# Another order for the opening of a spectral and gated-ReLU kernel

## The chip, the cores and the metric

The kernel runs on one core of one Trainium2 chip. The metric is the device time of one execution in microseconds (us), the median of several runs. A profiled execution gives a trace of every instruction on the five engines: TensorE (PE, with its weight loads as PEld), VectorE (DVE), ScalarE (ACT), GpSimd (POOL) and SyncE (SP), which here issues nearly all transfers. An engine works its instructions in the order in which the program has them, and each may wait on semaphores for others.

## The reference

For one sequence of 2048 rows of 448 numbers, the result is the input plus two branches, both on the layer-normalized rows:

```python
def _A_ref(x, w_r, w_i):
    X = jnp.fft.rfft2(x, axes=(-2, -1))
    X = X * (w_r + 1j * w_i)
    return jnp.fft.irfft2(X, s=(S, D), axes=(-2, -1))

def _B_ref(x, W_gate, W_up, W_down):          # W_gate, W_up: 448 x 1792, W_down: 1792 x 448
    gate = jnp.einsum("bsd,df->bsf", x, W_gate)
    up = jnp.einsum("bsd,df->bsf", x, W_up)
    gate = gate * (gate > 0)
    return jnp.einsum("bsf,fd->bsd", gate * up, W_down)

xn = _layernorm(x, axis=-1)
return x + _A_ref(xn, A_w_r, A_w_i) + _B_ref(xn, B_W_gate, B_W_up, B_W_down)
```

Everything is float32. The kernel keeps that precision with float16 matmuls: each operand is split into a high half (the value rounded to float16) and a low half (the rest), and a product is the sum of high x high, high x low and low x high.

## The kernel before

**Rows.** A tile is 128 rows, number `n2` of 16 (row 16 p + n2 on partition p). A chunk is four of them, `q`, `q + 4`, `q + 8`, `q + 12`; the chunks are taken in the order 0, 2, 1, 3. Each row tile is loaded (`load_xr`, "lx"), its mean and variance are taken on VectorE (`ln_stats`, "st": BN_STATS and BN_AGGR), the root on ACT (`ln_sd`, "sq"), and the reciprocal of the root with one refining step as four or five tiny operations on VectorE (`ln_rstd`, "rs"). In the two first chunks VectorE writes the normalized row in float32 (`ln_xn`, "xn", line 290) and also its low half (`ln_lo`, "lo", lines 324 and 325). The high half (`ln_hi`, "hi") is made by ACT; in chunk 0 straight from the raw row (line 297), in chunk 2 from the normalized one (line 299). GpSimd copies a few columns into place (`ln_copy`, "cp", and the last line of `ln_lo`, line 326). Chunk 0 is then transposed by TensorE against an identity (`ln_tp`, "tpA" and "tpB", line 344) and emptied into the tile T by VectorE (line 352, "vev") or ACT (line 350, "aev"). The other chunks are transposed by transfers (`ln_dma`, "dm", line 334), a transfer for each row tile; these go through SP's queue.

**Weights.** Gate and up weights come in 14 pairs `f`; each pair has two slabs, `g` = 0 (gate) and 1 (up), of 128 columns. A slab is loaded ("lw"), squared and summed by ACT (`w_sq`, "wsq", line 186), summed over the partitions by GpSimd (`w_sum`, "par", line 189), scaled by a power of two worked out by two tiny VectorE operations (`w_scale`, "wsc", lines 192 and 196), rounded to its high half by ACT (`w_hi`, "whi", line 690) and given its low half by VectorE (`w_lo`, "wlo", line 694). The down weights go the same way ("lwd", "wdq", "wdp", "wdsc", "wdh", "wdl").

**Units.** A unit is one `f` for one chunk: 20 full matmuls of 128x512 (line 740), ten to a slab, and two half passes (line 747). Two units in turn share their half passes: `gu_halves` ("hp") ends unit `f` and opens its mate, the next unit. Then come the relu on ACT ("re", line 777), the product on VectorE ("tm", line 781), and the high and low half of h ("gh", line 785, and "gl", line 789). A unit needs its PSUM tile, one of two, to be emptied by "tm" of the unit two before. When the five units of a group are done for a chunk, the matmuls with the down weights follow (line 808). The spectral branch (lines 368, 398, 639, 658 and VectorE's butterflies) is laid among the units by a planner with a list of costs.

**What sets the order.** The opening, all work up to the first chunk's five units, is written by hand: the string `OPENING` names some 280 pieces, and `manual_schedule` holds every engine to the order in which they are named. Unit 0 runs there in slabs of half a chunk (256 columns: "hh", "hl", "lh" with the slab and the half), as rows come in. `keep_warm` runs matmuls on a tile of zeros at the start and between early pieces ("warm", "kw1", "kw3", "kw6"). From there on a planner and the scheduler set the order.

Of the kernel before, what the change touches and what calls it, by code (L numbers as in the profile page):

```python
# [25 lines left out]
NWARM = 19  # L26
# [4 lines left out]
lx0 lx4 lw lid lw lx8 lx12 lw lw lw lw lx2 lx10 lx6 lx14 lwd0 lwd1 lwd2 lwd3 lwd4 warm st0 st4 sqA rsA hi4  # L31
xn4 xn0 wsqW0g0 cp4 st8 hi0 parW0g0 st12 wsqW0g1 cp0 tpA0 lo0 tpA4 kw1 wscW0g0 sqB tpB0 kw6 parW0g1 wsqW1g0
rsB whiW0g0 vevB0 lo4 wsqW1g1 xn12 tpB4 kw3 hi8 parW1 wscW0g1 xn8 whiW0g1 cp8 vevA0 vevA4 hi12 tpA8 vevB4
hh10 hh00 lo8 wsqW2g1 cp12 tpA12 hl00 lo12 aevA12 tpB8 aevA8 hl10 wloW0g0 lw aevB8 tpB12 wscW1 lh00 aevB12
wloW0g1 lw lfd hh01 hh11 whiW1g0 st2 lh01 lh10 whiW1g1 hl01 wloW1g0 lw hl11 wsqW2g0 wloW1g1 lw ly0 ly4 ly8
ly12 d90 d94 d98 d912 lh11 wsqW3g0 st10 parW2 hp0 st14 wsqW3g1 gu1g0 st6 wdq0 parW3 wscW2 sqC wscW3 whiW2g0 rsC gu1g1 re0
wloW2g0 whiW3g1 tm0 whiW2g1 xn6 wsqW4g0 xn2 gu2g0 wloW2g1 hi2 re1 xn10 gh0 wloW3g1 whiW3g0 tm1 gu2g1 wdq1
wloW3g0 hi10 xn14 lo2 hi14 hi6 cp14 hp2 wsqW4g1 cp2 lo6 gu3g0 cp10 dm2 lo14 re2 parW4 wdq2 cp6 wscW4 tm2
whiW4g0 dm14 lo10 wdq4 gu3g1 wloW4g0 gh1 dm10 gl0 whiW4g1 gl1 dm6 gu4g0 re3 wloW4g1 wdq3 tm3 wdp gh3
wdsc gh2 gu4g1 gl2 wdh1 wdh2 wdl1 wdh0 wdl2 hp4 gl3 re4 wdh3 tm4 wdl0 gh4 wdh4 gl4 wdl3 wdl4  # L40
# [105 lines left out]
def tile_gfnet_reglu(ctx: ExitStack, tc: tile.TileContext, x, xr, wgu, wd, wf, ident, c_fd, c_fm, c_im, c_row, c_id,  # L146
# [100 lines left out]
    def ln_stats(q, j):  # L247
        n2 = q + 4 * j
        st = ft([128, 6], F32, "bst", 2)
        V.bn_stats(st, xr_t[n2])  # L250
        if j == 0:
            mv[q] = ft([128, 4, 2], F32, "mv", 2)
        V.bn_aggr(mv[q][:, j, :], st)

    rst = {}

    def ln_sd(q, js=(0, 1, 2, 3)):
        w = ft([128, 5, 4], F32, "rs", 3)
        n = len(js)
        rst[q, js[0]] = w[:, :, 0:n], mv[q][:, js[0]:js[-1] + 1, :]  # L260
        A.activation(w[:, 0, 0:n], rst[q, js[0]][1][:, :, 1], AF.Sqrt, bias=eps)

    def ln_rstd(q, js=(0, 1, 2, 3), bias=False):
        w, m = rst[q, js[0]]
        sd, r0, t, r, nm = (w[:, i] for i in range(5))
        V.reciprocal(r0, sd)
        V.scalar_tensor_tensor(t, m[:, :, 1], 1e-5, r0, op0=OP.add, op1=OP.mult)
        V.scalar_tensor_tensor(t, t, -0.5 * 2048, r0, op0=OP.mult, op1=OP.mult)
        V.scalar_tensor_tensor(r, t, 1.5 * 2048, r0, op0=OP.add, op1=OP.mult)
        if bias:  # L270
            V.scalar_tensor_tensor(nm, m[:, :, 0], -1.0, r, op0=OP.mult, op1=OP.mult)
        elif q in CHUNKS[2:]:
            V.tensor_scalar(nm, m[:, :, 0], -1.0, None, op0=OP.mult)
        for i, j in enumerate(js):
            rst[q, j] = r[:, i:i + 1], nm[:, i:i + 1], m[:, i, 0:1]
# [9 lines left out]

    def ln_xn(n2):
        xn_b[n2] = free.pop(0)
        xn[n2] = xn_b[n2].rearrange("p g c k -> p (g c k)")[:, 0:D]
        r, _, mean = rst[n2 % 4, n2 // 4]
        V.tensor_scalar(xn[n2], xr_t[n2], mean, r, op0=OP.subtract, op1=OP.mult)  # L290

    def ln_hi(n2, fused=False):
        new_tt(n2)
        o = tt[n2].rearrange("p a b -> p (a b)")[:, 0:D]
        r, nm, _ = rst[n2 % 4, n2 // 4]
        if fused:
            A.activation(o, xr_t[n2], AF.Identity, scale=r, bias=nm)
        else:
            A.activation(o, xn[n2], AF.Copy)
# [6 lines left out]
    def ln_norm(n2):  # L306
        xn_b[n2] = free.pop(0)
        xn[n2] = xn_b[n2].rearrange("p g c k -> p (g c k)")[:, 0:D]
        r, nm, _ = rst[n2 % 4, n2 // 4]
        A.activation(xn[n2], xr_t[n2], AF.Identity, bias=nm)  # L310
        new_tt(n2)
        A.activation(tt[n2].rearrange("p a b -> p (a b)")[:, 0:D], xn[n2], AF.Copy, scale=r)
        ln_copy(n2)
        free.append(xr_b.pop(n2))

    def ln_lo(n2):
        x, t = xn[n2], tt[n2].rearrange("p a b -> p (a b)")
        x2, t2 = [v[:, None, :].to_broadcast([128, 2, 64]) for v in (x[:, 384:448], t[:, 384:448])]
        if n2 % 4 in CHUNKS[2:]:
            r = rst[n2 % 4, n2 // 4][0]  # L320
            V.scalar_tensor_tensor(t[:, 512:896], x[:, 0:384], r, t[:, 0:384], op0=OP.mult, op1=OP.subtract)
            V.scalar_tensor_tensor(tt[n2][:, 3:9:5, 64:128], x2, r, t2, op0=OP.mult, op1=OP.subtract)
        else:
            V.tensor_tensor(t[:, 512:896], x[:, 0:384], t[:, 0:384], op=OP.subtract)
            V.tensor_tensor(tt[n2][:, 3:9:5, 64:128], x2, t2, op=OP.subtract)
# [370 lines left out]
    def wd_sq(i, f):  # L696
        if i == 0:
# [45 lines left out]
    def gu_half(f, q, g, start, prev):  # L743
# [479 lines left out]
```

## Time and profile before

| | us |
|---|---|
| median of 3 runs | 447.49 (447.28 to 447.83) |
| the profiled execution: its own time | 448.09 |
| the profiled execution: span of its instructions | 446.3 |
| TensorE busy | 437.7 (98% of the span) |
| VectorE busy | 381.9 (86%) |
| ACT busy | 188.2 (42%) |
| granted TensorE clock, mean | 0.999 of full speed |

A row of the order of time reads: start, duration, engine, line and operation, tile written <- tiles read, shapes, how many in a row, and in brackets the idle time of the engine before it with what ended it. A row of a group reads: line, engine, operation, tiles, shapes, count, then busy time in all and the mean of one in ns, then idle time before. A row of windows gives each engine's busy time in a stretch with its count of instructions, the granted clock, the share of the transfer engines and GB/s. Instructions on one engine overlap a little at their ends, so a step from one to the next is some 0.05 to 0.1 us shorter than a duration.

### The profile page before, as it was taken

Reading aid. Unit: us, or ns where it says so; the run is one execution under the profiler, and the core shown is the slowest. Engines: PE = TensorE matmul, PEld = TensorE weight load, DVE = VectorE, ACT = ScalarE, POOL = GpSimd, SP = SyncE. Lnnn points to the kernel's source line nnn. Section 1 sums busy time; section 2 is a strip of 40 time slices with the busy share of each in tenths; the row PEclk is TensorE's granted clock in tenths of the full one; section 3 lists DMA queues with packets and bytes.
Section 4 is the critical chain, followed back from the end, with each engine's and each line's share of the span. In section 5 each row is a group of like instructions: output and inputs, shape, how many; then the busy total and the mean of one; then the engine's idle time right before and its main releaser. Section 6 shows DMA issues by size and latency. Waiting matters only on the chain.

```text
span 446.3 us, 7350 instructions
## 1 busy us (share of the span) xinstructions
PE 437.7 (98%) x2625; PEld 219.1 (49%) x2625; DVE 381.9 (86%) x958; ACT 188.2 (42%) x398; POOL 34.3 (8%) x89
## 2 busy tenths in 40 slices
PE   6999999999999999999999999999999999999996
PEld 2544555545455444444444444444445555555654
DVE  5989698999858899999999999987998799875443
ACT  5887263732643774323132255263334133244130
POOL 2320030210000310000000310100000000000000
PEclk9999999999999999999999999999999999999999
DMA  7939985040001462431302100011121121101212
GB/s 248 312 88 269 368 266 116 16 92 2 1 2 48 140 198 81 133 117 45 98 29 85 41 0 2 0 43 63 41 71 35 58 79 35 53 13 50 82 47 82
DMA packets 39228, 39.61 MB, mean 89 GB/s; under 512 B 18470, under 2 KB 35096, under 8 KB 39192
## 3 DMA queue, kind: packets, MB, share of 16 engines
q1 hardware_dynamic: 39192, 39.15, 28.6%
q8 instruction: 20, 0.33, 0.3%
q14 instruction: 16, 0.13, 0.1%
HBM read 24.38 MB, written 3.67 MB: 63 GB/s over the span
## 4 chain that ended last, share of the span: by engine, by line
PE 91%; DMA 3%; DVE 3%; issue 1%; SPq 0%; ACT 0%; POOL 0%; DVEq 0%; ACTq 0%
PE gu L740 51%; PE dn L808 26%; PE gu L747 3%; PE fx L639 2%; PE fx L368 2%; PE fx L658 2%; DMA wst<-in_wgu 2%; PE fx L398 2%; DMA y<-in_xr 1%; PE dn L836 1%; DVE wt L694 1%; PE gu L836 1%; DVE g L781 0%; DVE y L290 0%; DVE xy L814 0%
## 5 line engine op out<-in xcount | busy, mean ns | idle before, releaser
L740 PE MATMUL gu<-T,wt 128*128 128x512 f16 (+1 forms) x1140 | 255.6, 375 | 0.2 <-DVE wt L694 0.2
L740 PEld LDWEIGHTS <-wt 128*128 128x128 f16 x1140 | 108.7, 98 | 130.7 <-issue 9.8
L808 PE MATMUL dn<-wdt,h 128*128 128x448 f16 x624 | 127.0, 352 | 0.0
L808 PEld LDWEIGHTS <-h 128*128 128x128 f16 x624 | 60.3, 98 | 56.4 <-issue 0.4
L777 ACT ACTIVATE g<-gu 128x512 f32<-128x512 f32 x56 | 33.2, 593 | 92.4 <-PE gu L747 54.3
L785 ACT ACTIVATE h<-g 128x512 f16<-128x512 f32 x56 | 34.9, 626 | 58.2 <-DVE g L781 58.1
L781 DVE SCALAR_TENSOR_TENSOR g<-gu,g 128x512 f32<-128x512 f32 x56 | 38.3, 684 | 15.3 <-ACT g L777 15.2
L789 DVE TENSOR_TENSOR h<-g,h 128x512 f16<-128x512 f32 x56 | 38.3, 685 | 8.2 <-ACT h L785 8.0
L814 DVE SCALAR_TENSOR_TENSOR xy<-dn,dsc,xy 128x448 f32<-128x448 f32 x46 | 31.0, 676 | 12.3 <-PE dn L808 7.8
L189 POOL PARTITION_ALL_REDUCE wm<-wm x15 | 11.7, 779 | 167.8 <-ACT junk L186 167.8
L623 ACT ACTIVATE vt<-y,fsc 128x456 f16<-128x456 f32 x16 | 10.8, 673 | 27.9 <-PE fx L639 23.7
L690 ACT ACTIVATE wt<-wst,wsc 128x512 f16<-128x512 f32 x28 | 19.3, 714 | 5.6 <-DVE wsc L196 5.6
L694 DVE SCALAR_TENSOR_TENSOR wt<-wst,wsc,wt 128x512 f16<-128x512 f32 x28 | 20.4, 744 | 0.0
L186 ACT ACTIVATE junk<-wst 128x512 bf16<-128x512 f32 x28 | 17.4, 621 | 0.2
L747 PE MATMUL gu<-T,wt 64*128 64x512 f16 x112 | 17.0, 381 | 0.1
L663 DVE SCALAR_TENSOR_TENSOR xy<-fx,fsc,xy 128x448 f32<-128x448 f32 x16 | 10.8, 680 | 7.2 <-PE fx L658 7.2
L389 ACT ACTIVATE Xh<-X 128x456 f16<-128x456 f32 x16 | 9.3, 579 | 17.7 <-DVE X L387 8.7
L404 DVE TENSOR_TENSOR y<-y,y 128x456 f32<-128x456 f32 x22 | 13.8, 627 | 0.2
L639 PEld LDWEIGHTS <-vt 128*128 128x128 f16 x192 | 12.0, 98 | 4.0 <-issue 0.8
L250 DVE BATCH_NORM_STATS2 bst<-y 128x6 f32<-128x448 f32 x16 | 9.7, 612 | 4.9 <-DMA y<-in_xr 4.9
L405 DVE TENSOR_TENSOR y<-y,y 128x456 f32<-128x456 f32 x22 | 13.8, 626 | 0.1
L639 PE MATMUL fx<-im,vt 128*128 128x128 f16 x192 | 13.5, 219 | 0.0
(131 smaller groups left out, 476.9 us busy)
## 6 DMA issues: line engine op xcount, KB each, us to landing
sw<-y SPq DMA_DIRECT2D x64, 112.2 KB
wst<-in_wgu SPq DMA_DIRECT2D x28, 256.0 KB
wf<-in_wf SPq DMA_DIRECT2D x16, 228.0 KB
y<-in_xr SPq DMA_DIRECT2D x16, 224.0 KB
xy<-in_x SPq DMA_DIRECT2D x16, 224.0 KB
out<-xy SPq DMA_DIRECT2D x15, 224.0 KB
wdst<-in_wd SPq DMA_DIRECT2D x14, 224.0 KB
fm<-in_c_fm SPq DMA_DIRECT2D x4, 256.0 KB
```

The lines of the kernel that those rows point to most:

```text
L186: A.activation(mt([128, 512], BF16, "junk")[:, 0:src.shape[-1]], src, AF.Square, scale=SQ, accum_out=acc)
L639: P.matmul(o, v[:, h, w], m[:, c, :], start=(i == 0), stop=(i == 2), skip_group_check=True)
L690: A.activation(w[:, 0:4, :], wst[f, g], AF.Copy, scale=wsc[f, g])
L694: V.scalar_tensor_tensor(w[:, 4:8, :], st, sc, w[:, 0:4, :], op0=OP.mult, op1=OP.subtract)
L740: last["P"] = P.matmul(hps[f, q][:, g, cs], wt[f, g][:, a, :], Tq[q][:, b, cs], start=(start and i == 0), stop=(stop and i == len(seq) - 1 ...
L747: m = P.matmul(hps[f, q][:, g, 0:512], wt[f, g][rows, 7, :], Tq[q][rows, b, :], start=start, stop=not start).ins
L777: last["A"] = A.activation(g1s[f, q], hps[f, q][:, 0, :], AF.Relu, scale=2.0 ** -22).ins
L781: last["V"] = V.scalar_tensor_tensor(g1, hps[f, q][:, 1, :], 2.0 ** -22, g1, op0=OP.mult, op1=OP.mult).ins
L785: A.activation(ht[f, q][:, 0, :], g1s[f, q], AF.Copy)
L789: V.tensor_tensor(h[:, 1, :], g1s.pop((f, q)), h[:, 0, :], op=OP.subtract)
L808: last["P"] = P.matmul(ps[:, 0:D], ht[f, q][:, a, js], wdt[f][:, b, :], start=(i == 0), stop=(i == n - 1)).ins
L814: last["V"] = V.scalar_tensor_tensor(xy[:, n2, cs], dps[n2][:, cs], dsc[:, g:g + 1], xy[:, n2, cs], op0=OP.mult, op1=OP.add).ins
```

## The change

The opening string is replaced by another of much the same work, with smaller pieces. What differs:

- Row tiles 0, 4, 12 and 8 are loaded before any weight slab. The identity is loaded by ACT's queue, ahead of its table load, and no longer by SP's.
- Statistics are two pieces ("bn", "ag"), the root's refining four ("ra" to "rd"), and the low half of a row two ("lo", 384 columns, and "lp", 128 columns). The power of two of a weight slab is two pieces ("wex", "wsc").
- Rows 0 and 4, half of chunk 0, are centred by ACT ("xc": row minus mean, float32), and their high half is made by ACT from that with the scale. Their low half on VectorE multiplies by the scale in the same operation. Rows 8 and 12 are normalized by VectorE as chunk 2 is. The mean's negative ("ng") is made before the root.
- Unit 1, the mate of unit 0, is run in six pieces: for each slab high x high ("uh"), the part with low rows ("um") and low x high ("ul"). The half passes that it shares with unit 0 lie inside and neither open nor close it.
- 24 warm-up matmuls at the start and 4 between ("kw4"), for 19 and 10.
- Chunks 1 and 3, in the planner's part, take statistics two rows at a time.

```diff
-NWARM = 19
+NWARM = 24
 OPENING = """
-lx0 lx4 lw lid lw lx8 lx12 lw lw lw lw lx2 lx10 lx6 lx14 lwd0 lwd1 lwd2 lwd3 lwd4 warm st0 st4 sqA rsA hi4
...
+lx0 bn0 warm lx4 bn4 ag0 ag4 lx12 ngA lx8 sqA raA xc4 lw lw lw rbA ly8 xc0 rcA rdA bn12 ag12 hi4 lo4 cp4 lx2 hi0
+tpA4 bn8 aevA4 wsqW0g0 lp4 ag8 lo0 tpA0 lx10 vevA0 parW0g0 lw sqB raB lp0 wsqW0g1 parW0g1 rbB lw wsqW1g0 wexW0g0
...
+    def ln_neg(q, js=(0, 1, 2, 3)):
+        t = ft([128, 4], F32, "nm", 3)[:, 0:len(js)]
+        V.tensor_scalar(t, mv[q][:, js[0]:js[-1] + 1, 0], -1.0, None, op0=OP.mult)
...
+    def ln_xc(n2):
+        xn_b[n2] = free.pop(0)
+        xn[n2] = xn_b[n2].rearrange("p g c k -> p (g c k)")[:, 0:D]
+        A.activation(xn[n2], xr_t[n2], AF.Identity, bias=rst[n2 % 4, n2 // 4, "m"])
...
-    def ln_hi(n2, fused=False):
+    def ln_hi(n2):
         new_tt(n2)
-        o = tt[n2].rearrange("p a b -> p (a b)")[:, 0:D]
-        r, nm, _ = rst[n2 % 4, n2 // 4]
-        if fused:
-            A.activation(o, xr_t[n2], AF.Identity, scale=r, bias=nm)
-        else:
-            A.activation(o, xn[n2], AF.Copy)
+        if n2 in whole:
+            A.activation(tt[n2].rearrange("p a b -> p (a b)")[:, 0:D], xn[n2], AF.Copy)
+            return
+        A.activation(tt[n2].rearrange("p a b -> p (a b)")[:, 0:D], xn[n2], AF.Copy, scale=rst[n2 % 4, n2 // 4])
...
+    def ln_lo1(n2):
+        t = tt[n2].rearrange("p a b -> p (a b)")
+        if n2 in whole:
+            V.tensor_tensor(t[:, 512:896], xn[n2][:, 0:384], t[:, 0:384], op=OP.subtract)
+            return
+        V.scalar_tensor_tensor(t[:, 512:896], xn[n2][:, 0:384], rst[n2 % 4, n2 // 4], t[:, 0:384], op0=OP.mult,
+                               op1=OP.subtract)
...
     def gu_halves(f, q, mate):
-        gu_open(*mate)
+        inside = mate in hps
+        if not inside:
+            gu_open(*mate)
         m = last["P"]
         for i in range(4):
             with tc.high_priority(offset=2000 if i else 0):
-                m = gu_half(*((f, q) if i > 1 else mate), 1 - i % 2, i < 2, m)
+                m = gu_half(*((f, q) if i > 1 else mate), 1 - i % 2, i < 2 and not inside, m, i > 1)
...
-    pieces = {"lid": lambda: nc.sync.dma_start(id_t, ident), "lfd": lambda: nc.sync.dma_start(fd_t, c_fd),
+    pieces = {"lid": lambda: nc.scalar.dma_start(id_t, ident), "lfd": lambda: nc.sync.dma_start(fd_t, c_fd),
...
+    def gu_part(g, n):
+        if (1, q) not in hps:
+            gu_open(1, q)
+        gu_full(1, q, (g,), slice(0, 512), n == 0, n == 2, (seq1[0:3], seq2, seq1[3:6])[n])
```

How it moves instructions is shown at three places. In the rows below a tile's name has its buffer's number behind it: y1_67 and y0_66 are rows 4 and 0 as loaded, y2_68 and y3_69 rows 12 and 8 after the change and rows 8 and 12 before it.

ACT, from the first root to the second slab's rounding. Before:

```order
L261 ACTIVATE rs_172<-mv_167,eps_92 128x2
L297 ACTIVATE tt0_100<-y1_67,rs_172 128x448
L186 ACTIVATE junk_183,wm_182<-wst_117 128x512
L297 ACTIVATE tt1_101<-y0_66,rs_172 128x448
L186 ACTIVATE junk_195,wm_182<-wst_120 128x512
L261 ACTIVATE rs_214<-mv_167,eps_92 128x2
L186 ACTIVATE junk_229,wm_228<-wst_124 128x512
L690 ACTIVATE wt_236<-wst_117,wsc_211 128x512
```

and after the change:

```order
L269 ACTIVATE rs_154<-mv_147,eps_92 128x2
L311 ACTIVATE y4_70<-y1_67,nm_151 128x448
L311 ACTIVATE y5_71<-y0_66,nm_151 128x448
L325 ACTIVATE tt0_100<-y4_70,rs_154 128x448
L325 ACTIVATE tt1_101<-y5_71,rs_154 128x448
L382 ACTIVATE T0_62<-fx_178 128x3x128
L187 ACTIVATE junk_186,wm_185<-wst_158 128x512
L269 ACTIVATE rs_201<-mv_147,eps_92 128x2
L187 ACTIVATE junk_206,wm_185<-wst_160 128x512
L187 ACTIVATE junk_213,wm_212<-wst_162 128x512
L727 ACTIVATE wt_232<-wst_158,wsc_230 128x512
```

Two centrings stand ahead of the two high halves, and an evacuation of a transpose (L382) stands ahead of the first weight square.

VectorE, around the low half of the first weight tile (L694 before, L731 after). Before:

```order
L352 COPY T0_62<-fx_206 128x5x128
L324 TENSOR_TENSOR tt2_102<-y11_77,tt2_102 128x384
L325 TENSOR_TENSOR tt2_102<-y11_77,tt2_102 128x2x64
L324 TENSOR_TENSOR tt3_103<-y10_76,tt3_103 128x384
L325 TENSOR_TENSOR tt3_103<-y10_76,tt3_103 128x2x64
L694 SCALAR_TENSOR_TENSOR wt_236<-wst_117,wsc_211,wt_236 128x512
```

and after the change:

```order
L317 TENSOR_SCALAR y9_75<-y3_69,mv_147,rs_201 128x448
L384 COPY T0_62<-fx_192 128x5x128
L731 SCALAR_TENSOR_TENSOR wt_232<-wst_158,wsc_230,wt_232 128x512
L341 TENSOR_TENSOR tt3_103<-y9_75,tt3_103 128x384
L350 TENSOR_TENSOR tt3_103<-y9_75,tt3_103 128x2x64
L341 TENSOR_TENSOR tt2_102<-y8_74,tt2_102 128x384
L350 TENSOR_TENSOR tt2_102<-y8_74,tt2_102 128x2x64
L384 COPY T0_62<-fx_266 128x3x128
```

The weight tile's low half now stands ahead of the low halves of rows 8 and 12, and an evacuation (L384, of row 8) stands behind them.

GpSimd, at the end of the opening: the copies for chunk 2's rows (tt0 to tt3), the reductions for the last gate and up weights (wm) and for the down weights (wdm). Before:

```order
L189 ISA wm_441<-wm_441 128x2
L303 COPY tt3_103<-tt3_103 128x48
L304 COPY tt3_103<-tt3_103 128x64
L326 COPY tt1_101<-tt1_101 128x48
L189 ISA wdm_404<-wdm_404 128x5
```

and after the change:

```order
L354 COPY tt3_103<-tt3_103 128x48
L354 COPY tt2_102<-tt2_102 128x48
L354 COPY tt1_101<-tt1_101 128x48
L190 ISA wdm_116<-wdm_116 128x5
L329 COPY tt1_101<-tt1_101 128x48
L330 COPY tt1_101<-tt1_101 128x64
```

The last row tile's two copies (tt1, row 2), which its transposing transfer needs, now stand behind the reduction of the down weights.

More of the change, by code (lines that the diff above doesn't have):

```diff
@@ L257, in ln_sd @@
+    bst, rst, whole = {}, {}, set()
     def ln_sd(q, js=(0, 1, 2, 3)):
-        w = ft([128, 5, 4], F32, "rs", 3)
         n = len(js)
-        rst[q, js[0]] = w[:, :, 0:n], mv[q][:, js[0]:js[-1] + 1, :]
-        A.activation(w[:, 0, 0:n], rst[q, js[0]][1][:, :, 1], AF.Sqrt, bias=eps)
-    def ln_rstd(q, js=(0, 1, 2, 3), bias=False):
-        w, m = rst[q, js[0]]
[L265 to L273, printed above, removed]
+        w = ft([128, 5, 4], F32, "rs", 3)[:, :, 0:n]
+        rst[q, js[0]] = w, mv[q][:, js[0]:js[-1] + 1, :]
+        A.activation(w[:, 0], mv[q][:, js[0]:js[-1] + 1, 1], AF.Sqrt, bias=eps)
@@ L741, in gu_full, with gu_half @@
                                      start=(start and i == 0), stop=(stop and i == len(seq) - 1)).ins
-    def gu_half(f, q, g, start, prev):
+    def gu_half(f, q, g, start, prev, stop):
         rows, b = TOP[g]
-        m = P.matmul(hps[f, q][:, g, 0:512], wt[f, g][rows, 7, :], Tq[q][rows, b, :], start=start, stop=not start).ins
+        m = P.matmul(hps[f, q][:, g, 0:512], wt[f, g][rows, 7, :], Tq[q][rows, b, :], start=start, stop=stop).ins
         if "opened" in state:
@@ L853, in ln_chunk @@
     def ln_chunk(q):
-        for j in range(4):
-            add(0.63, ln_stats, q, j)
+        for js in ((0, 1), (2, 3)):
+            add(1.24, ln_stats, q, js)
         add(0.0, ln_sd, q)
+        add(0.1, ln_neg, q)
         add(0.6, ln_rstd, q)
@@ L1080, in gu_slab @@
     def gu_slab(f, g):
-        if f % 2 == 0 and g == 0:
+        if (f, q) not in hps:
             gu_open(f, q)
         gu_full(f, q, (g,), slice(0, 512), f % 2 == 0, f % 2 == 1)
+    def gu_part(g, n):
+        if (1, q) not in hps:
+            gu_open(1, q)
+        gu_full(1, q, (g,), slice(0, 512), n == 0, n == 2, (seq1[0:3], seq2, seq1[3:6])[n])
+    for g in range(2):
+        for n, t in enumerate(("uh", "um", "ul")):
+            piece(f"{t}{g}", gu_part, g, n)
     for f in groups[0]:
@@ L1113, in tile_gfnet_reglu @@
         gu_open(0, q)
+        state["wdm"] = mt([128, 2, NR], F32, "wdm", 1)
         for name in OPENING.split():
```

114 lines of the change are left out of this document (69 added, 45 removed).

## The prediction

> **What bounds the kernel now.** I read the busy line first, then busy time by window, then TensorE's waits, then the order of time on TensorE up to 40 us.
>
> ```profile
> PE 437.7 (98%) x2625; PEld 219.1 (49%) x2625; DVE 381.9 (86%) x958; ACT 188.2 (42%) x398; POOL 34.3 (8%) x89
> ```
> ```profile
> core 0: us, PE busy (x) PEld busy (x) DVE busy (x) ACT busy (x) POOL busy (x), PEclk, DMA share, GB/s
> 8.00:10.40 2.40, 0.72 (x7) 0.39 (x7) 1.97 (x6) 1.36 (x5) 0.55 (x3) 1.00 1.01 356
> 16.09:34.60 18.51, 18.30 (x105) 9.06 (x102) 16.96 (x46) 16.71 (x39) 4.94 (x17) 1.00 0.55 150
> 39.00:443.00 404.00, 403.52 (x2436) 202.49 (x2432) 349.64 (x861) 158.69 (x333) 24.06 (x49) 1.00 0.25 76
> ```
> ```profile
> engine line waited for: us in total, times, longest us
> PE fx L344 <- DVE tt L324: 1.7, 2, 1.3
> PE dn L1054 <- POOL warm L1111: 1.5, 1, 1.5
> PE fx L344 <- ACT tt L297: 0.7, 1, 0.7
> PE fx L344 <- ACT wt L690: 0.5, 1, 0.5
> PE gu L740 <- DVE wt L694: 0.2, 1, 0.2
> ```
> ```profile
> 1.54 6.10 PE L1054 MATMUL dn<-warm 128*128 128x512 f16 x19 [1.54 <-POOL warm L1111]
> 10.75 1.46 PE L1054 MATMUL dn<-warm 128*128 128x512 f16 x6
> 14.44 0.81 PE L740 MATMUL gu<-T,wt 128*128 128x256 f16 x6
> 20.51 8.81 PE L740 MATMUL gu<-T,wt 128*128 128x512 f16 x40
> 29.25 0.61 PE L747 MATMUL gu<-T,wt 64*128 64x512 f16 x4
> 34.66 4.28 PE L740 MATMUL gu<-T,wt 128*128 128x512 f16 x19 [0.17 <-DVE wt L694]
> 38.87 0.61 PE L747 MATMUL gu<-T,wt 64*128 64x512 f16 x4
> ```
>
> From 39 to 443 us TensorE is busy for 403.52 of 404.00 us, so the end is set by when it reaches the work that starts there. All its waits lie in the opening. The first useful slab (a pass over one weight tile) runs at 14.44. After that one wait is left, 0.2 us at 34.66, on VectorE's low half of a weight tile (L694). That small wait matters most: it says that VectorE and TensorE reach the last unit of the first chunk together. An earlier first slab is worth nothing by itself, unless VectorE too gets there earlier. The marker I use is the row at 38.87, the half passes that end the first chunk's five units and touch the second chunk (hp4): every microsecond by which it comes earlier comes off the total, as long as the rest stays gapless.
>
> **The start.** The rows are normalized first; their prices are all in the trace.
>
> ```profile
> 3.37 0.63 DVE L250 BATCH_NORM_STATS2 bst<-y 128x6 f32<-128x448 f32 x1 [2.50 <-DMA y<-in_xr]
> 4.98 0.30 ACT L261 ACTIVATE rs<-mv,eps 128x2 f32<-128x2 f32 x1 [2.75 <-DVE mv L253]
> 15.09 0.33 PE L344 MATMUL fx<-id_t,tt 128*128 128x128 f16 x3
> 15.46 0.49 ACT L350 ACTIVATE T<-fx 128x384 f16<-128x384 f16 x1
> L310 ACT ACTIVATE y<-y,rs 128x448 f32<-128x448 f32 x8 | 4.7, 655 | 0.0
> L312 ACT ACTIVATE tt<-y,rs 128x448 f16<-128x448 f32 x8 | 4.8, 659 | 1.8 <-DVE rs L269 1.8
> L186 ACT ACTIVATE junk<-wst 128x512 bf16<-128x512 f32 x10 | 6.2, 620 | 0.1
> L690 ACT ACTIVATE wt<-wst,wsc 128x512 f16<-128x512 f32 x10 | 7.0, 719 | 1.6 <-DVE wsc L196 1.6
> 12.80 0.64 POOL L189 PARTITION_ALL_REDUCE wm<-wm  x1
> ```
>
> Rows 0 and 4 still arrive first, so the square root stays near 4.9. Centring on ACT (the form of L310, 0.66) runs beside VectorE's four small steps instead of behind them: two centrings and two roundings (L312, 0.66) end at about 4.9 + 0.3 + 4 x 0.57 = 7.5, since back-to-back steps overlap by some 0.09. But 24 warm-up matmuls instead of 19 stand ahead of the first transpose: 7.64 + 5 x 0.216 (six took 1.46 with a 0.38 tail) = 8.7. So the earlier rounding buys nothing there, and ACT, whose next instruction empties that transpose, stands idle for some 1.5 us. Its copy starts 0.37 after the transposes (15.09 to 15.46), at 9.1. Behind it in ACT's order stand the copy 0.49, three weight squares of 0.62 + 0.19 and the second square root 0.30, less overlaps, 2.7 in all: the first weight rounding starts at 11.8 and ends 0.72 later at **12.5**, against 14.44. The 1.9 us come from the order: before, the first slab took the second weight tile, for whose rounding TensorE stood 0.5 us (the wait on ACT wt L690); now it takes the first, and rows 0 and 4 are out of PSUM by then. The first weight slab is now loaded fifth instead of third, but is wanted only at 9.5; the identity, issued by ACT ahead of its table load, at 8.7. Both moves cost nothing.
>
> The TensorE work from the first slab to the end of unit 1 is the same pieces in other order: 24.83 (half of the 40 matmuls from 20.51) less 14.44 is 10.4, and 0.3 for the second weight rounding, due at 14.2: unit 1 ends at 12.5 + 10.7 = 23.2. TensorE is 1.6 us ahead there. Splitting unit 1 into pieces adds no matmul.
>
> **VectorE's path.** The low half of the first weight tile (wloW0g0) begins a stretch in which VectorE hardly rests.
>
> ```profile
> 16.09 0.74 DVE L694 SCALAR_TENSOR_TENSOR wt<-wst,wsc,wt 128x512 f16<-128x512 f32 x1
> 30.10 0.56 DVE L324 TENSOR_TENSOR tt<-y,tt 128x384 f16<-128x384 f32 x1 [0.50 <-ACT tt L299]
> 32.32 0.17 DVE L192 TENSOR_SCALAR eg<-wm 128x2 uint32<-128x2 uint32 x1 [0.67 <-POOL wm L189]
> 33.86 0.74 DVE L694 SCALAR_TENSOR_TENSOR wt<-wst,wsc,wt 128x512 f16<-128x512 f32 x1
> 32.72 0.72 ACT L690 ACTIVATE wt<-wst,wsc 128x512 f16<-128x512 f32 x1 [1.00 <-DVE wsc L196]
> L324 DVE TENSOR_TENSOR tt<-y,tt 128x384 f16<-128x384 f32 x8 | 4.4, 554 | 0.5 <-ACT tt L299 0.5
> L325 DVE TENSOR_TENSOR tt<-y,tt 128x128 f16<-128x128 f32 x8 | 2.3, 292 | 0.0
> L352 DVE COPY T<-fx 128x640 f16<-128x640 f16 x2 | 1.0, 480 | 0.0
> L352 DVE COPY T<-fx 128x384 f16<-128x384 f16 x2 | 0.6, 344 | 0.0
> L789 DVE TENSOR_TENSOR h<-g,h 128x512 f16<-128x512 f32 x3 | 2.0, 684 | 0.0
> ```
>
> Before, from that tile (16.09) to the low half of W4g0, which releases the last unit (33.86 + 0.74 = 34.60), are 18.51 us: 16.96 busy and 1.55 idle, of which 0.50 and 0.67 are the two waits shown and 0.38 small gaps. After, the same stretch holds the same 46 instructions and more: the low parts of rows 8 and 12 now stand inside it (2 x (0.55 + 0.29) = 1.69), three evacuations moved in, two of them from ACT (0.34 + 2 x 0.48 = 1.30), and one low half of h (0.68) stands ahead of W4g0. Together 3.67, less 0.05 overlap for each of the eight, 3.3: the stretch has 20.2 us of work.
>
> Its start: the weight tile is ready at 12.5, but wloW0g0 stands behind the centring of row 8 and an evacuation of row 0. That needs GpSimd's copy of row 0, which now stands behind the all-reduce for the second weight tile: square done 11.1, all-reduce to 11.7 (0.64 where it met other work), two copies 12.1, transposes, and the evacuation ends at 13.35. The stretch ends at 13.35 + 20.2 = 33.55 with no idle time. I take 0.2 for gaps, half of the small ones of before, because the two long waits lose their ground: in ACT's new order the squares and roundings of W4 stand ahead of three of the five squares of the down weights, its first rounding comes at about 29.7 by the count of what precedes it instead of 32.72, and the reduction that VectorE waited for at 32.32 is done by then. So 33.75, and from there to hp4 the 20 matmuls as before (38.87 less 34.62 is 4.25): **38.0**. TensorE itself would be there at 37.4: by the same count hp2's half passes wait for wloW3g0 until 28.3 and end at 28.8, and two units of 4.3 follow.
>
> Sum: 38.87 - 38.0 = 0.9 us. Bounds: with no gap, and the stretch begun right at 12.55, 37.0, a gain of 1.9; with the whole idle time of before (1.55), 13.35 + 20.2 + 1.55 + 4.25 = 39.35, a loss of 0.5. One warm-up matmul fewer is idle filler and counts nothing. Chunks 1 and 3 get their statistics in pairs, under TensorE's cover: nothing, or 0.2 a time if the cover is gone.
>
> The profiled execution took 448.09 with a span of 446.3; a span of 445.4 should follow. The median before is 447.49, 0.6 below the profiled one, so the median after is **446.6**.
>
> **The rivals.**
>
> *VectorE rests as long as before.* Then the stretch ends at 35.1 and the time is 448.0, slower. For it: VectorE now waits in order for a second square root that stands on ACT behind the evacuation and a square, an idle of 0.9 at 9.4 to 10.4 that I counted, and such waits may recur later where each small step is its own piece. Against it: ACT runs some 3 us ahead of its old dates from 25 us on. It decides from 1.1 us of idle time in the stretch. Chance 0.14.
>
> *The second chunk's transposes arrive last.*
>
> ```profile
> 30.79 6.02 SPq L334 DMA_TRANSPOSE T<-tt  x4
> 36.55 0.45 POOL L189 PARTITION_ALL_REDUCE wdm<-wdm  x1 [2.52 <-ACT junk L186]
> ```
>
> hp4 reads the second chunk's T. The four issues fill 30.79 to 36.81, 1.5 each, so the last begins at about 35.3; its reader starts at 38.87, so one takes at most 3.5. In the new order row 2's two GpSimd copies stand behind the down weights' all-reduce, itself behind three squares on ACT. From hp2's end (about 28.8): relu and two roundings to 31.0, three squares to 33.0, reduce 33.6, copies 34.1, transpose 37.6. That is 0.4 under the 38.0 of the sum. If re2 is late by 1 us it takes the lead, at 38.5: 447.1, no change to be told. Chance 0.20, with other small slips that eat half the gain.
>
> *The stretch begins earlier.* If loads and all-reduce leave the evacuation of row 0 by 12.6, VectorE ends at 33.0, the transposes lead at 37.6 and the time is 446.2. For it: the reduction that I took at 0.64 ran beside two of GpSimd's copies, and the one at 36.55, alone, took 0.45. Chance 0.17.
>
> *TensorE's clock falls.* The granted clock is 1.00 in every window, also from 8.0 to 10.4 where TensorE was busy 0.72 of 2.40. Now the filler ends at 8.7 + transposes + 4 x 0.22, about 10.1, and up to 12.5 only five transposes run. If that gap throttles, matmuls take 0.43 instead of 0.22 for as long as the first warm-up did (1.54 to about 5.3), a loss of 1.9: hp4 at 39.6 and 448.2. Chance 0.07. [...]
>
> **How the numbers follow.** What two measurements of this kernel can tell apart is about 0.2%, 0.9 us: 446.6 is just at that edge. The forecast has a chance of 0.42, half of it on either side of that edge, a little more on the faster one (0.25); the earlier start (0.17) is faster and takes with it a few hundredths of the slips. The rest of the slips stays within 0.2%. VectorE's idling and the clock are slower, with part of the former within 0.2%. So faster 0.46, same 0.37, slower 0.17. The range 445.5 to 448.0 takes in both bounds of VectorE's stretch (gain 1.9, loss 0.5); outside it are the clock and what the planner may make of the body.
>
> **What would show it.** Right: first slab near 12.5, the low half of W0g0 near 13.4, that of W4g0 ending near 33.8 with TensorE waiting for it or arriving with it, hp4 near 38.0, no gap behind it, and a span of 445.4. Wrong: a granted clock under 1.00 between 10 and 18 us; idle time of VectorE over 1.1 us from 13.4 to 34; hp4 released by a transpose; or TensorE idle more than 0.5 us behind 39, which would mean that the body, not the opening, set the difference.

## The result

The changed kernel takes 452.28 us (median of 4 runs, 451.2 to 452.6) against 447.51 (447.28 to 447.83) before: a ratio of 1.0102, 95% interval 1.0083 to 1.0120. It is slower by 1.0%, where 446.6 was forecast. The profiled execution took 452.6 with a span of 450.8, 4.5 more than the 446.3 of before.

TensorE is busy for longer, though it does the same work; the busy line of the page of the change:

```profile
PE 440.5 (98%) x2624; PEld 219.9 (49%) x2624; DVE 381.5 (85%) x957; ACT 187.8 (42%) x398; POOL 39.6 (9%) x89
```

GpSimd's 34.3 us have become 39.6 for the same instructions, and TensorE's 437.7 have become 440.5. TensorE in order of time, the change (start, length, engine and line, operation, count, and in brackets the idle time ahead and what ended it):

```profile
1.54 8.06 PE L1094 MATMUL dn<-warm 128*128 128x512 f16 x24 [1.54 <-POOL warm L1162]
9.43 0.50 PE L376 MATMUL fx<-id_t,tt 128*128 128x128 f16 x6
13.23 0.50 PE L777 MATMUL gu<-T,wt 128*128 128x256 f16 x3 [0.43 <-ACT wt L727]
29.74 8.81 PE L777 MATMUL gu<-T,wt 128*128 128x512 f16 x40
40.81 0.72 PE L784 MATMUL gu<-T,wt 64*128 64x512 f16 x4 [2.27 <-DMA T<-tt]
41.47 6.01 PE L777 MATMUL gu<-T,wt 128*128 128x512 f16 x20
```

The last two rows hold most of the loss. The half passes that touch the second chunk (hp4) start at 40.81, 1.94 later than before, and TensorE had nothing to do for 2.27 us ahead of them: it waited for the second chunk's transposes. The 20 matmuls behind them took 6.01 us, where the same 20 took 4.49 before; that is 1.5 more. Before:

```profile
39.41 4.49 PE L740 MATMUL gu<-T,wt 128*128 128x512 f16 x20
```

The windows of the change show why, in the column of the granted clock (the last but two):

```profile
38.55:40.81 2.26, 0.00 (x0) 0.03 (x1) 2.26 (x5) 0.87 (x2) 0.00 (x0) 1.00 0.80 170
41.25:44.50 3.25, 3.25 (x10) 1.10 (x9) 2.25 (x4) 2.19 (x4) 0.00 (x0) 0.50 1.00 311
44.75:47.50 2.75, 2.75 (x14) 1.25 (x13) 0.00 (x0) 0.00 (x0) 0.00 (x0) 1.00 1.06 391
```

The clock was 1.00 in the gap, fell to 0.50 soon behind it, at about 41.2, stayed there for some 3.4 us, and was back at 1.00 from 44.75. Of the remaining 1.0 us of the span, 0.6 is one later wait of TensorE and 0.1 the half passes themselves (0.72 for 0.61); in the other 0.3 TensorE is busy longer with the same 343 matmuls (54.49 for 54.16 up to the run below), for a reason that I did not find. All of it arises ahead of a run of 20 matmuls that starts at 102.55 after and at 98.06 before (first row before, second after); from there the two traces run 4.49 us apart to the end.

```profile
98.06 4.48 PE L740 MATMUL gu<-T,wt 128*128 128x512 f16 x20
```
```profile
102.55 4.48 PE L777 MATMUL gu<-T,wt 128*128 128x512 f16 x20
PE fx L400 <- DVE y L474: 0.6, 1, 0.6
```

Why were the transposes late? GpSimd, VectorE and SP's queue in order of time, the change:

```profile
29.79 2.76 POOL L329 COPY tt<-tt 128x48 f16<-128x48 f16 x1
32.49 0.23 POOL L330 COPY tt<-tt 128x64 f16<-128x64 f16 x1
32.67 0.22 POOL L354 COPY tt<-tt 128x48 f16<-128x48 f16 x1
```
```profile
29.78 0.28 DVE L350 TENSOR_TENSOR tt<-y,tt 128x128 f16<-128x128 f32 x1
29.98 0.68 DVE L828 TENSOR_TENSOR h<-g,h 128x512 f16<-128x512 f32 x1
30.58 1.01 DVE L341 TENSOR_TENSOR tt<-y,tt 128x384 f16<-128x384 f32 x2
31.52 0.48 DVE L350 TENSOR_TENSOR tt<-y,tt 128x128 f16<-128x128 f32 x2
31.92 0.55 DVE L341 TENSOR_TENSOR tt<-y,tt 128x384 f16<-128x384 f32 x1
32.39 0.68 DVE L820 SCALAR_TENSOR_TENSOR g<-gu,g 128x512 f32<-128x512 f32 x1
32.91 5.84 SPq L366 DMA_TRANSPOSE T<-tt  x4
```

A GpSimd copy of 48 columns, 0.22 us at its best, took 2.76. All that time VectorE ran, with no gap, operations that read both operands from SBUF (rows y and tt, gates g and h). The copy ended 0.16 us after VectorE turned to L820, which reads one operand from PSUM. It is the first of row 14's copies. In GpSimd's order only row 6's first two stand ahead of it, so all those behind it were late, and the four transposes, which go out one after the other (5.84 us for four), were issued from 32.91 instead of 30.79. The trace alone shows a coincidence; the runs below test it.

### The profile page after: what moved, and what is told of

Its sections match the earlier page's. It is cut to its first block, busy times and chain, and to the rows that moved or that the text cites. A ratio compares the mean times of both kernels' runs of the same rounds, so it can differ in the third digit from the quotient of the medians.

```text
span 450.8 us, 7343 instructions
## 1 busy us (share of the span) xinstructions
PE 440.5 (98%) x2624; PEld 219.9 (49%) x2624; DVE 381.5 (85%) x957; ACT 187.8 (42%) x398; POOL 39.6 (9%) x89
## 4 chain that ended last, share of the span: by engine, by line
PE 91%; DVE 4%; POOL 1%; DMA 1%; ACT 1%; issue 1%; SPq 0%; DVEq 0%; POOLq 0%
PE gu L777 49%; PE dn L847 26%; PE gu L784 3%; PE fx L671 2%; PE fx L690 2%; PE fx L400 2%; PE fx L430 2%; PE dn L1094 2%; PE dn L875 1%; DVE wt L731 1%; DMA T<-tt 1%; DVE bst L250 1%; DMA y<-in_xr 1%; PE gu L875 1%; POOL tt L329 1%
## 5 line engine op out<-in xcount | busy, mean ns | idle before, releaser
L820 DVE SCALAR_TENSOR_TENSOR g<-gu,g 128x512 f32<-128x512 f32 x56 | 38.4, 686 | 21.0 <-ACT g L816 20.9
L190 POOL PARTITION_ALL_REDUCE wm<-wm x15 | 13.9, 933 | 174.7 <-ACT junk L187 174.7
L731 DVE SCALAR_TENSOR_TENSOR wt<-wst,wsc,wt 128x512 f16<-128x512 f32 x28 | 20.5, 745 | 0.3 <-issue 0.2
L329 POOL COPY tt<-tt 128x48 f16<-128x48 f16 x16 | 8.7, 541 | 55.7 <-ACT tt L325 28.1
```

Of the source, the lines that this page charges most:

```text
L731: V.scalar_tensor_tensor(w[:, 4:8, :], st, sc, w[:, 0:4, :], op0=OP.mult, op1=OP.subtract)
L820: last["V"] = V.scalar_tensor_tensor(g1, hps[f, q][:, 1, :], 2.0 ** -22, g1, op0=OP.mult, op1=OP.mult).ins
```

## The experiments

Theory **A**: GpSimd's copies are held up while VectorE runs two-SBUF-input operations back to back; so the transposes come late; and the idle time this makes lowers the clock. The rivals: **B**, SP's queue or the transposes' own chain is late; **C**, row 2's copies behind the all-reduce of the down weights; **D**, the clock falls for another reason; **F**, anything that reads SBUF is slowed; **G**, the statistics in pairs cost time in the body. All ratios are to the kernel before on the same chip.

**One VectorE instruction moved.** In the order table, tm2 (a gate, PSUM source) goes ahead of lo10:

```diff
-hi10 lo10 re2 dm14 whiW4g0 whiW4g1 ... wdq4 lo2 tm2 wdq3
+hi10 re2 tm2 lo10 dm14 whiW4g0 whiW4g1 ... wdq4 lo2 wdq3
```

> One VectorE instruction moves: tm2, which reads PSUM, stands ahead of lo10 instead of behind lo2 and so breaks the run of operations with two SBUF inputs at about 30.6 us instead of 32.4. Theory A (GpSimd's copies are held up while VectorE runs two-SBUF-input operations back to back, the transposes follow late, and the gap then lowers the granted clock): the copy of row 14 ends inside tm2, by 31.3 instead of 32.55, the first transpose is issued at 31.2 to 31.6 instead of 32.91, the wait in front of the half passes is 0.5 to 0.9 us instead of 2.27, they start at 39.0 to 39.4, and the clock holds: 449.2, or 450.7 if the clock falls all the same. Rival B (the transposes are late through SP's own queue or their serial chain): first issue at 32.9, 452.3. Rival C (row 2's copies behind the down weights' all-reduce set the last transpose): the first three issues come earlier, the fourth stays at 37.3, 452.3.

Measured: 449.3 us, ratio 1.0042 (1.0026 to 1.0058). VectorE, then GpSimd:

```profile
29.68 0.68 DVE L820 SCALAR_TENSOR_TENSOR g<-gu,g 128x512 f32<-128x512 f32 x1
```
```profile
28.89 0.95 POOL L329 COPY tt<-tt 128x48 f16<-128x48 f16 x1
29.79 0.23 POOL L330 COPY tt<-tt 128x64 f16<-128x64 f16 x1
29.96 0.22 POOL L354 COPY tt<-tt 128x48 f16<-128x48 f16 x1
30.13 0.22 POOL L329 COPY tt<-tt 128x48 f16<-128x48 f16 x1
30.29 2.18 POOL L330 COPY tt<-tt 128x64 f16<-128x64 f16 x1
```

```profile
39.38 0.61 PE L784 MATMUL gu<-T,wt 64*128 64x512 f16 x4 [1.74 <-DMA T<-tt]
```

The copy again ends 0.16 us after the moved operation starts, three more slip through while it runs, and the next, too late for it, is held for 2.18 us by the run that follows. The first transpose is issued at 30.21, the wait at hp4 is 1.74 and the clock stays at 1.00. Rivals B and C fall: neither SP nor the order of the all-reduce was touched. (In the change itself row 2's copies end at 35.59, and its transpose starts at 37.3, behind the three before it.) The wait shrank less than expected, since the other three rows' copies were held up in their turn. Of the 2.8 us by which this profile's span is shorter than that of the change, about 0.9 is another thing: its filler ended earlier, and its first slab ran at 12.33 (below). The shorter wait gives about 0.5 and the clock 1.5.

**The gap filled.** Ten warm-up matmuls stand ahead of hp4:

```diff
-wdl0 dm2 gu4g1 hp4
+wdl0 dm2 gu4g1 kw10 hp4
```

> Ten warm-up matmuls (2.2 us) stand ahead of the half passes that wait for the transposes; nothing else changes. Theory A (the idle gap lowers the granted clock): half passes still start at 40.8 to 41.0, the granted clock is 1.00 from 40 to 45, and the 20 matmuls behind them take 4.5 us instead of 6.0: 450.9 (450.7 to 451.2). Rival D (the clock falls for another reason, such as the load of the opening): the clock still falls to 0.6 or 0.7, 452.3.

Measured: 450.72 us, 1.0066 (1.0050 to 1.0082), clock 1.00 in all four runs.

```profile
37.23 2.32 PE L1094 MATMUL dn<-warm 128*128 128x512 f16 x10
39.59 0.61 PE L784 MATMUL gu<-T,wt 64*128 64x512 f16 x4
40.13 4.49 PE L777 MATMUL gu<-T,wt 128*128 128x512 f16 x20
```

The 20 matmuls take 4.49 again, and 1.6 us come off the median: without the gap the clock did not fall (D falls). In this execution everything stands 1.2 us earlier, which comes from the first 10 us (below); the copy still took 2.77.

**The second chunk's copies on ACT**, in the same places of the order, low parts' copies too:

```diff
+        if n2 in (2, 6, 10, 14):
+            A.activation(t[:, 7, 0:48]..., t[:, 0:3, 112:128], AF.Copy)
+            A.activation(t[:, 7, 64:128], t[:, 3, 0:64], AF.Copy)
+            return
         G.tensor_copy(t[:, 7, 0:48]..., t[:, 0:3, 112:128])
```

> The second chunk's twelve small copies (rows 2, 6, 10, 14) are made by ACT instead of GpSimd; 12 x about 0.2 = 2.4 us more of ACT's time between 28 and 36. Theory A (GpSimd alone is locked out): ACT's copies take 0.2 us each beside VectorE's dense run, the first transpose is issued at 30.5 to 31.5, the wait in front of the half passes is under 0.7 us, no fall of the clock, 448.7 to 449.8; VectorE may wait up to 1 us for ACT's later rounding of the fifth weight tile. Rival F (any second reader of SBUF is held up by VectorE): ACT's copies take 1 to 2.7 us as GpSimd's did, and nothing is gained: 452 to 453. Rival B: transposes at 32.9 as before, 452.3.

Measured: 448.38 us, 1.0009 (0.9999 to 1.0019). Beside the same dense VectorE work ACT's copies take 0.23 us, so F falls:

```profile
31.47 0.23 ACT L330 ACTIVATE tt<-tt 128x48 f16<-128x48 f16 x1
38.32 0.61 PE L792 MATMUL gu<-T,wt 64*128 64x512 f16 x4 [0.73 <-DVE h L836]
```

By the ratios the loss shrinks from 1.02% to 0.09%. In the profile some 1 us of that is an earlier filler once more (first slab at 12.01). And hp4 still waits 0.73: the row names VectorE, but the last transpose was issued at 34.8, 3.5 ahead of hp4, as in the change (37.3) and with tm2 moved (35.9), so the transposes most likely still release it.

**The held copy by itself** (one execution), behind the opening: a GpSimd copy becomes ready, then VectorE runs a chain of a known kind.

```diff
+        for t, (n, kind) in enumerate(((4, "ss"), (8, "ss"), (8, "ps"), (8, "s"), (8, "tick"))):
+            V.tensor_scalar(lc, la, 0.0, None, op0=OP.mult)
+            G.tensor_copy(lg[:, 48 * t:48 * t + 48], lc[:, 400:448])
+            for i in range(n): ...   # V.tensor_tensor(ld, la, lb), (ld, wps, lb) or V.tensor_scalar(ld, la)
```

> A measurement by itself, behind the opening: five times a GpSimd copy (128x48, f32) becomes ready and VectorE then runs a chain of independent operations of 448 elements: 4 and 8 with two SBUF inputs, 8 with one PSUM and one SBUF input, 8 with one SBUF input, and 8 with two SBUF inputs and a tiny operation on PSUM behind the second. VectorE is some 20 us later for it, so its time (455 to 475) says nothing. Theory A (GpSimd is locked out by VectorE's operations with two SBUF inputs until the chain is broken): the copy takes as long as the chain lasts, about 2.2 and 4.4 us, 0.2 to 0.5 us beside the PSUM chain and the one-input chain, and about 1.3 us where the tiny operation stands. Rival (the 2.76 us copy was slow by itself, or by its form): all five take 0.2 to 0.6 us. Rival (it waits for one VectorE operation only): 0.5 to 0.8 us in both first chains.

The scheduler mixed the chains with the body's own operations, so each of the five copies is read by what VectorE really ran beside it. Three of them:

```profile
64.19 1.31 POOL L1175 COPY y<-y 128x48 f32<-128x48 f32 x1 [12.51 <-DVE y L1174]
72.36 0.32 POOL L1175 COPY y<-y 128x48 f32<-128x48 f32 x1 [6.86 <-DVE y L1174]
76.46 0.62 POOL L1175 COPY y<-y 128x48 f32<-128x48 f32 x1 [3.77 <-DVE y L1174]
```
```profile
64.03 0.28 DVE L416 TENSOR_TENSOR X<-eo 128x114 f32<-128x114 f32 x1
64.22 0.64 DVE L424 TENSOR_TENSOR Xh<-X,Xh 128x456 f16<-128x456 f32 x1
...
65.33 1.29 DVE L1178 TENSOR_TENSOR y<-dn,y 128x448 f32<-128x448 f32 x2
...
72.22 2.10 DVE L1180 TENSOR_SCALAR y<-y 128x448 f32<-128x448 f32 x5
...
76.31 0.69 DVE L828 TENSOR_TENSOR h<-g,h 128x512 f16<-128x512 f32 x1
76.91 0.64 DVE L1182 TENSOR_TENSOR y<-y,y 128x448 f32<-128x448 f32 x1
```

The copy at 64.19 was held through five two-input operations, until the one from PSUM began (1.31). Beside five one-input operations back to back it took 0.32: density alone does not hold it. The one at 76.46 got in behind a single two-input operation (0.62), although another followed at once. The two not shown fit: 0.22 beside an operation that reads PSUM (51.46), and 0.55 beside one two-input operation with nothing behind it (45.88). So the copy may be held through a whole run, and is not always; the expected 4.4 us and 1.3 us of the long chains were not seen in this form. What ends a hold stays open. It need not be an operation from PSUM: with tm2 moved, the copy of 2.18 us ended 0.18 us after VectorE began L731 at 32.29, which reads two operands from SBUF too. The rows show whose copies slow down, GpSimd's (2.76 us in the change) and not ACT's (0.23 in the same place), and beside what; why a hold can last over several VectorE instructions is not shown.

**The warm-up's length.** 19 matmuls instead of 24 at the start:

```diff
-NWARM = 24
+NWARM = 19
```

> The change with 19 warm-up matmuls instead of 24. In the profiled execution of the change the filler ended at 9.60 and held the first transposes to 9.43, in later executions of the same opening they came at 8.2 to 8.5, as the filler's pace rose at another time. If the filler sets the start: first transposes at 7.4 to 8.4 whatever the pace, the first slab 0.3 to 0.9 us earlier than beside 24, unit 1 too; but the half passes behind the second chunk's transposes move only as far as GpSimd's copies do, so 0.3 to 0.9 us off 452.3: 451.4 to 452.0, with the gap and the clock's fall still there. If another engine sets the start (rows, statistics): nothing, 452.3.

Measured: 450.94 us, 1.0066 (1.0050 to 1.0082), better than expected: by its mean (0.996 against 0.999 and 1.000) the clock fell in two of its four runs only. In its profile 19 matmuls took 7.05 us, while 24 took 6.93 in the run with the filler and 8.06 in the profile of the change, and in all three the transposes start as the filler ends (first fence: 19 matmuls; second: the run with the filler ahead of hp4):

```profile
1.54 7.05 PE L1094 MATMUL dn<-warm 128*128 128x512 f16 x19 [1.54 <-POOL warm L1162]
8.43 0.50 PE L376 MATMUL fx<-id_t,tt 128*128 128x128 f16 x6
```
```profile
1.54 6.93 PE L1094 MATMUL dn<-warm 128*128 128x512 f16 x24 [1.54 <-POOL warm L1162]
28.59 8.81 PE L777 MATMUL gu<-T,wt 128*128 128x512 f16 x40
```

The matmuls start at half pace: in the change's profile the first seven take 3.17 us, 0.45 each, and in the run with the filler the ten later ones 2.32, 0.23 each. (The column of the granted clock reads 1.00 from the start, so it does not show this.) The moment at which the pace rises differs between executions: in five profiles with this opening the 24 matmuls end between 8.26 and 9.60. Before, the first transposes waited for ACT anyway (0.73 us); the new order hands this chance to everything behind it.

**Statistics one at a time again**, on top of the ACT copies:

```diff
-        for js in ((0, 1), (2, 3)):
-            add(1.24, ln_stats, q, js)
+        for j in range(4):
+            add(0.63, ln_stats, q, (j,))
```

> The second chunk's copies on ACT, as in the run before (448.4), and the statistics of chunks 1 and 3 one row at a time again, as before the change, instead of in pairs. Theory G (the pair puts a row's statistics on VectorE some microseconds ahead of that row's load, with butterflies and gates queued behind: VectorE waited 4.15 us for the load in the change at 71 us, and TensorE 0.58 us for a butterfly at 77; 1.0 in the run with filler): VectorE's wait for the load at 70 to 76 falls under 1.5 us, no TensorE wait on a butterfly, and 0.3 to 1.0 us come off: 447.4 to 448.1. Rival (TensorE's cover holds, the pairs cost nothing): 448.4.

Measured: 448.16 us, 1.0012 (1.0003 to 1.0022), against 1.0009. No gain is seen, and VectorE still waits for the row's load (first row: pairs; second: singly). A cost under some 0.5 us is within the two intervals.

```profile
71.85 0.63 DVE L250 BATCH_NORM_STATS2 bst<-y 128x6 f32<-128x448 f32 x1 [2.94 <-DMA y<-in_xr]
```
```profile
71.11 0.63 DVE L250 BATCH_NORM_STATS2 bst<-y 128x6 f32<-128x448 f32 x1 [2.56 <-DMA y<-in_xr]
```

So theory G finds no support. Neither of these two profiles has TensorE's wait on that VectorE operation (L474 in the change), and the first of the better versions below, with single statistics, has it (0.4). Why the body's order puts these statistics ahead of their load, and whether that is what stops TensorE for 0.2 to 1.0 us in some profiles, stays open.

**Only the two costs removed**, the held copies and the long filler: the ACT copies as above, with the statistics in pairs again, and

```diff
-NWARM = 24
+NWARM = 14
```

> The change with only its two suspected costs removed: the second chunk's copies on ACT in place (which gave 448.38), and 14 warm-up matmuls instead of 24; everything else stays. If these two make up the loss: first slab 0.3 to 1.2 us earlier than beside 24, less spread, 446.8 to 447.6, no slower than before. If more is lost elsewhere in the opening: 448.0 to 448.6.

Measured: 446.82 us, 0.9981 (0.9971 to 0.9992). With the copies and the filler mended, the change is no longer slower but 0.2% faster than before.

**A better version, step by step.** First the copies on ACT right behind the roundings, those of the low parts on VectorE, row 6's low part ahead of gl0 and its transpose second, 19 warm-up matmuls, statistics singly:

```diff
-hi14 wloW3g1 ... hi2 hi6 cp6 ... cp14 ... lp14 gl0 ... lo6 lp10 lp6 ... wdp cp2
+hi14 cp14 wloW3g1 ... hi2 cp2 hi6 cp6 ... lp14 lo6 lp6 gl0 ... lp10 ... wdp
```

> All of it together: the second chunk's copies on ACT right behind the roundings and, those behind the low parts, on VectorE; row 6's low part ahead of gl0; 19 warm-up matmuls; statistics one by one. If each cost is what the theories say: first slab at 11.7 to 12.3, first transpose of the second chunk issued by 29, the four at most 1.5 us apart, half passes at 37.3 to 38.0 with no wait on a transpose, no fall of the clock, 446.2 to 447.0 against 447.5 of before. If VectorE's longer stretch (four copies of some 0.1 us more) or ACT's takes the lead: half passes at 38.3 to 39.0, 447.2 to 448.0.

Measured: 446.55 us, 0.9971 (0.9961 to 0.9981); hp4 at 37.64 with no wait. Then 14 warm-up matmuls:

```diff
-NWARM = 19
+NWARM = 14
```

> The best version so far (446.55 against 447.76) with 14 warm-up matmuls instead of 19. The rounded rows stand ready at 7.1 us, the filler held the first transposes to 8.56. If the filler alone holds them: transposes at 7.1 to 7.4, first slab 0.5 to 1.2 us earlier (11.2 to 11.9), half passes 0.3 to 1.2 earlier, 445.4 to 446.3. Rival (the clock: with fewer matmuls ahead the pace rises later and the transposes and slabs run at half pace, or the second square root and row 8's statistics hold the first slab anyway): 446.3 to 448.

Measured: 445.92 us, 0.9956 (0.9942 to 0.9969); transposes at 7.34, first slab at 11.57, hp4 at 36.85. With 19 matmuls and the copies of rows 12 and 8 on VectorE instead:

```diff
-        G.tensor_copy(t[:, 7, 0:48]..., t[:, 0:3, 112:128])
+        e = V if n2 in (8, 12) else G
+        e.tensor_copy(t[:, 7, 0:48]..., t[:, 0:3, 112:128])
```

> The best version so far with the copies of rows 12 and 8 (on GpSimd the first took 2.17 us at 12.8) made by VectorE, ahead of and behind the first low half. Theory A: the transposes of row 8 and 12 that waited for them at 15.57 start 0.4 to 0.8 us earlier, VectorE's idle 0.92 us in front of the evacuation at 15.8 falls under 0.3, TensorE's wait on these copies goes, half passes 0.3 to 0.6 us earlier: 446.0 to 446.3. Rival (VectorE pays as much for the copies as it saves, or another wait takes its place): 446.4 to 446.9.

Measured: 446.51 us, 0.9967 (0.9955 to 0.9979): no gain by itself. The transposes do come sooner, and VectorE's idle 0.92 goes, but now TensorE meets VectorE's low half of the fifth weight tile:

```profile
33.04 4.27 PE L786 MATMUL gu<-T,wt 128*128 128x512 f16 x19 [0.35 <-DVE wt L740]
```

Both together:

> Both: 14 warm-up matmuls and rows 12 and 8 copied by VectorE. If they add up: half passes at 36.4 to 37.2 unless the second chunk's last transpose (landing at about 36.9 in the version before) or VectorE's low half of the fifth weight tile leads: 445.2 to 446.0. If one of these leads: 446.0 to 446.5.

Measured: 445.73 us, 0.9950 (0.9937 to 0.9964), the lowest of all, but not to be told from the 0.9956 with 14 matmuls alone. hp4 stands at 37.09, held by that low half (0.57): the limit is VectorE.

**The kernel before with the same repairs**, in the old order; ACT's copies as above, and

```diff
-NWARM = 19
+NWARM = 14
-        G.tensor_copy(tt[n2][:, 8, 0:48]..., tt[n2][:, 4:7, 112:128])
+        (V if n2 in (2, 6, 10, 14) else G).tensor_copy(tt[n2][:, 8, 0:48]..., tt[n2][:, 4:7, 112:128])
```

> The kernel before with the same repairs: the second chunk's copies on ACT, those behind its low parts on VectorE, 14 warm-up matmuls. If the new order itself is worth what the best version shows (445.7), the old order does not gain from them: its copies were short (0.22 to 0.57 us) and its first transposes waited for ACT, not for the filler; VectorE, which released its last unit, gets four copies more: 447.5 to 448.6. If the repairs alone are worth it: 446.0 to 446.8.

Measured: 448.01 us, 1.0003 (0.9994 to 1.0012). Nothing is gained there: the repairs alone are worth nothing, so the 2 us of the last version need the new order, rearranged so that nothing starves in it. (Here 14 matmuls may be too few: TensorE then idles 2.37 us ahead of the first transposes, and the mean clock was 0.992 to 0.996 in three of the ten runs. The parts were not tried singly.)

## Why the prediction was wrong

*Where TensorE is bound* was right: the end follows hp4, and all costs arose ahead of 102 us.

*The first slab at 12.5.* It ran at 13.23 in the profile of the change, and at 11.9 to 12.3 in four other executions of the same opening (the runs with tm2 moved, with the filler, with the copies on ACT, and with single statistics). The term that failed is the filler's end, 8.7: I added five warm matmuls to the 7.64 of one execution, as if that pace were fixed. It held for those four (8.3 to 8.7), but the change's own profile had 9.60. That the filler would hold the transposes and leave ACT idle was right.

*VectorE's stretch.*

```profile
13.71:33.93 20.22, 19.60 (x122) 10.45 (x122) 18.98 (x54) 18.70 (x45) 10.49 (x18) 1.00 0.55 156
```

From 13.71, against the 13.35 of the sum, it took 20.22 us, against 20.4. But that is luck, for two errors cancel: its work was 18.98, not 20.2, and its idle time 1.24, not 0.2. The eight instructions came in as counted (46 before, 54 now) but added 2.0 us and not 3.3; back to back they overlap more than the 0.05 that I took (two low parts of 0.55 take 1.01), which is a part of it. The 1.24 is over the 1.1 at which I let the rival decide that VectorE rests as long as before; with the work as I had priced it the stretch would have ended at 35.15, where that rival had it (35.1). Of the idle time 0.92 is one wait for transposes that stood behind another copy held up, 2.17 us at 13.70. The end, 33.93, was forecast at 33.75. That VectorE sets TensorE's last unit was not seen in the change, where the transposes came later still, but it is what bounds the last versions.

*hp4 at 38.0* failed by 2.8. TensorE was ready for it at 38.55, where 37.4 was forecast: that is the late filler, for in the run with ten matmuls ahead of hp4, where the first filler ended early, TensorE was ready at 28.59 + 8.81 = 37.40. The other 2.27 are the rival that the transposes arrive last, to which I gave a chance of 0.20 and 38.5. The place was right, the size was not. I let only row 2 be late, behind the all-reduce, and priced two copies at 0.5 us; what failed is that price, taken without regard to what VectorE runs beside them. Row 14's first copy alone took 2.76, the first of the four transposes slipped by 2.1 us, and they follow each other about 1.45 apart. GpSimd's rows of before had the warning:

```profile
15.31 0.23 POOL L326 COPY tt<-tt 128x48 f16<-128x48 f16 x1 [1.36 <-DVE tt L324]
16.21 0.70 POOL L326 COPY tt<-tt 128x48 f16<-128x48 f16 x1
```

The same copy takes 0.23 or 0.70. I passed over that, and did not ask how it would grow with VectorE's density, though a denser VectorE was my gain.

*The clock.* I had it fall in the opening's gap, 10.1 to 12.5, at a chance of 0.07. That chance was my estimate: the longest idle time of TensorE in the trace of before is 1.54 us, so nothing there showed what one of 2.4 does. In the opening the clock stayed at 1.00; it fell behind the gap of 2.27 at hp4, at a price of 1.5 where 1.9 was worked out. Two other runs have gaps of this length (first row: 19 matmuls; second: the old order repaired):

```profile
40.02 0.61 PE L784 MATMUL gu<-T,wt 64*128 64x512 f16 x4 [2.48 <-DMA T<-tt]
8.47 0.51 PE L352 MATMUL fx<-id_t,tt 128*128 128x128 f16 x6 [2.37 <-ACT tt L297]
```

Behind the gap of 2.27 the profiled clock fell to 0.50, and behind that of 2.48 it read 0.77 from 40 to 42.5 us and 0.55 from 42.5 to 45 (20 matmuls in 6.18 us); by the mean clock (0.996) it fell in three of four runs of the change, though a few executions of the kernel before have that mean too. Behind 1.74 it stayed at 1.00, and behind the 2.37 in the second row no fall is seen: six matmuls at 9.74 took 1.46 us, as long as six in the trace of before, and the mean clock of that execution is 0.999. So a gap of this length may cost the clock or not; what decides was not tested.

*The moves taken as free.* The identity, the weight slabs' order and the split of unit 1 show no wait of TensorE in the trace; none was undone alone. The pairs of statistics cost nothing that could be told. The body was not gapless: 0.6, over the 0.5 that the prediction named as a sign against it.

In sum: the gain forecast is there once the copies keep pace and the filler ends in time: 1.1 us with these two mended alone (447.89 to 446.82), and 2.0 us in the version that is rearranged as well (447.73 to 445.73). The change as made starves the copies.

## What to carry to other kernels

Before packing an engine's stretch, look for who worked beside it: here GpSimd's smallest copies did, and seven two-input operations of VectorE in a row held one of them for 2.76 us, which cost more than the packing gave. Where GpSimd feeds something critical, put a PSUM-source operation between VectorE's two-input ones (with tm2 moved the copy that had taken 2.76 us took 0.95, though a later one was held for 2.18), or give the copy to ACT (0.23). Size warm-up filler so that it ends before the work it stands ahead of even when its pace rises late: here 24 matmuls ended at 8.26 in one execution and at 9.60 in another.

## What the runs showed of the hardware

A 48-column GpSimd copy took 0.22 us, or up to 2.77, by what VectorE ran beside it; ACT's took 0.23 in the same place, and VectorE's own 0.17 (for rows 12 and 8). In two profiles the clock fell after TensorE had idled for 2.27 and 2.48 us (to 0.50 for some 3.4 us in the first, to 0.77 and 0.55 in two windows of 2.5 us in the second), and in one no fall is seen after 2.37. The first 24 matmuls ended between 8.26 and 9.60 in five executions of the same opening, as their pace rose earlier or later, and the first transposes, which stand behind them, started between 8.10 and 9.43.
